# Top-k attention followed by an MLP on one core: all queues in a fixed order, one more step between the stages, half-bank scores, MLP handed out matmul by matmul, centring folded into the first weight

## The chip, the cores and the metric

The kernel runs on one core of a Trainium2 chip. The metric is the device time of one execution in microseconds (us), as the median of several runs. TensorE (PE) does matrix products and transposes, PEld is its weight load, VectorE (DVE), ScalarE (ACT) and GpSimd (POOL) work element by element, and SyncE (SP) issues the DMAs.

## The reference

Two blocks follow each other, all in float32. B = 8 batches, H = 8 heads, S = 576 rows, D = 64 columns per head; the MLP is 512 wide with 2048 hidden columns.

```python
scores = scale * np.matmul(q, k.transpose(0, 1, 3, 2))
kth = np.partition(scores, -top_k, axis=-1)[..., -top_k:-top_k + 1]   # top_k = 32
scores = np.where(scores >= kth, scores, -1000000000.0)
attn = np.exp(scores - np.max(scores, axis=-1, keepdims=True))
attn = attn / (np.sum(attn, axis=-1, keepdims=True) + 1e-09)
x = heads_side_by_side(np.matmul(attn, v))          # (8, 576, 512)
mu, var = mean(x), mean((x - mu) ** 2)               # over the 512 columns
xn = (x - mu) / np.sqrt(var + 1e-06) * g_ln
out = x + np.maximum(xn @ w_ch1, 0.0) @ w_ch2
```

The two weights arrive as float64, which the chip does not compute with, so the kernel builds float32 values from the two 32-bit halves of each number.

## The kernel before

**Units.** Work comes in jobs (a batch and a pair of heads) and in units. A full unit is 128 query rows of both heads of a job; the fifth unit of a job (`rest`) is the last 64 rows of both heads, stacked in one 128-row tile. There are 32 (batch, head pair) combinations, so 160 units, 128 of them full. Batches 0 and 7 are split in two halves (rows 0 to 255, then the rest), each a job of its own, so there are 40 jobs.

**Stages of a unit.** `scores` multiplies queries and keys into two PSUM tiles of two banks each, and ACT copies each tile in one piece of 576 columns to `sc` (L276). `select` runs on DVE: four rounds of the eight largest values (`max`, L288), with three `match_replace` between them (L293). `mask` on POOL (L303, L306) pushes everything under the 32nd value far down. `weigh` is the exp on ACT (L313) with its row sum in `den`. `turn` transposes the weights on PE (L335, L354, L355, L363) and ACT copies them to `pt`. When a group of two or three units is done, `values` multiplies with v (L379), and `place` transposes the result back (L412) and ACT scales it by 1/`den` into the tile `x` (L414). For the `rest` unit the weights themselves are scaled instead (L329).

**MLP.** When a batch (or half) is complete, `mlp_items` gives a list of closures: `stats`, with mean and variance on DVE, the centred tile `xn` on POOL (L451) and its transpose; then 16 `hidden` items of four matmuls (L468); then per tile four `project` items of four matmuls (L483). `fill` pops them in the main loop, in five places per step, evenly over the steps until the next batch ends. The rest rows of two batches make one block of one tile.

**Weights.** `load_weight` handles 32 pieces of 128 x 512 numbers, two per step in the first 16 steps: five DVE operations (L133 to L143), three POOL operations (L135, L144, L146 or L149), one or two on ACT.

**What sets the order.** In step n of the main loop the code traces `scores` of unit n+1, `select` of unit n, `mask` and `weigh` of unit n-1, and `turn` of unit n-2 (and `values` and `place` if it ends a group). That is only a wish: when the program is closed, the framework's scheduler puts each engine's instructions into an order of its own by priority and its estimates. On the chip each engine then takes its queue in that order. PSUM has eight banks: four in `scps`, one in `tpps` for every transpose, three in `mmps` for the products.

Of the kernel before, what the change touches and what calls it, by code (L numbers as in the profile page):

```python
# [15 lines left out]
TOP_K = 32  # L16
# [4 lines left out]
J = 4  # L21
# [7 lines left out]
def kernel(  # L29
# [25 lines left out]

    nc = tc.nc
# [10 lines left out]

    def pool(name, bufs, **kw):
        return ctx.enter_context(tc.tile_pool(name=name, bufs=bufs, **kw))

    GQ = 2 * P + R

    consts = pool("consts", 1)
    ldpool = pool("ld", 2)
    rawpool = pool("raw", 1)
# [10 lines left out]
    xpool = pool("x", 9)  # L86
    rpool = pool("r", 2)
    rowpool = pool("row", 2)
# [3 lines left out]
    tpps = pool("tpps", 1, space=PSUM)  # L92
    mmps = pool("mmps", 3, space=PSUM)

    def const(shape, name):
        return consts.tile(shape, FP32, tag=name, name=name)

# [8 lines left out]
    def load_weight(i):  # L106

        if i < NF:
            c, n0 = i % NC, (i // NC) * DM
            src = w_ch1[c * P : (c + 1) * P, 2 * n0 : 2 * (n0 + DM)]
            dst = w1[:, c, n0 : n0 + DM]
        else:
            f = i - NF
            src = w_ch2[f * P : (f + 1) * P, :]  # L120
            dst = w2[:, f, :]
        raw = rawpool.tile([P, DM, 2], U32, tag="raw", name="raw")
        nc.sync.dma_start(raw[:].rearrange("p n w -> p (n w)"), src)
        lo, hi = raw[:, :, 0], raw[:, :, 1]

        def tmp(name):
            return hpool.tile([P, DM], U32, tag="h", name=name)

        size, sign, power = tmp("size"), tmp("sign"), tmp("power")
        low = hpool.tile([P, DM], FP32, tag="h", name="low")  # L130
        size_f = size[:].bitcast(FP32)
        nc.scalar.mul(low[:], lo, 2.0**-52)
        nc.vector.tensor_scalar(size[:], hi, 0x7FFFFFFF, None, ALU.bitwise_and)  # L133
        nc.vector.tensor_scalar(sign[:], hi, 0x80000000, None, ALU.bitwise_and)
        nc.gpsimd.tensor_scalar(size_f, size_f, HIGH_MAX, HIGH_MIN, ALU.min, ALU.max)  # L135
        nc.vector.tensor_scalar(
            size[:], size[:], 0x38000000, 3, ALU.bitwise_xor, ALU.logical_shift_left
        )
        nc.vector.scalar_tensor_tensor(
            out=size[:], in0=size[:], scalar=0x7FFFFFFF, in1=sign[:],  # L140
            op0=ALU.bitwise_and, op1=ALU.bitwise_or,
        )
        nc.vector.tensor_scalar(power[:], size[:], 0xFF800000, None, ALU.bitwise_and)  # L143
        nc.gpsimd.tensor_tensor(low[:], low[:], power[:].bitcast(FP32), ALU.mult)  # L144
        if i < NF:
            nc.gpsimd.tensor_tensor(low[:], size_f, low[:], ALU.add)  # L146
            nc.scalar.mul(dst, low[:], gcol[:, c : c + 1])
        else:
            nc.gpsimd.tensor_tensor(dst, size_f, low[:], ALU.add)  # L149

    def load_gain():
        grow = const([NC, P], "grow")
        nc.sync.dma_start(grow[:], g_ln.rearrange("(c p) -> c p", p=P))
        ps = tpps.tile([P, 512], FP32, tag="tp", name="gps")
        nc.tensor.transpose(ps[:, 0:NC], grow[:], ident[0:NC, 0:NC])
        nc.vector.tensor_copy(gcol[:], ps[:, 0:NC])

# [3 lines left out]
    slots = [0]  # L161
# [19 lines left out]
    def load(job):  # L181
        b, hp = job.b, job.hp
        ins = {}
        for name, src in (("k", k), ("q", q)):
# [7 lines left out]
            ins[name] = t  # L192
        vb = vpool.tile([P, 2 * J + 1, D], FP32, tag="v", name="vb")
        for hh in range(2):
            rows = v[b, 2 * hp + hh]
# [5 lines left out]
        ins["v"] = vb  # L201
        return ins

    def transpose_heads(ins):
        got = {}
        for name in "kq":
            dst = kqpool.tile([P, S], FP32, tag=name + "T", name=name + "T")
            ps = tpps.tile([P, 512], FP32, tag="tp", name="kqps")
            for c in range(J):
                nc.tensor.transpose(  # L210
                    ps[:, c * P : (c + 1) * P],
                    ins[name][:, c].rearrange("p h d -> p (h d)"),
                    ident[:],
                )
            if name == "k":
                nc.scalar.copy(dst[0:D, 0:JP], ps[0:D, :])
                nc.scalar.copy(dst[D:P, R:S], ps[D:P, :])
            else:
                nc.scalar.copy(dst[:, 0:JP], ps[:])
            got[name] = dst  # L220
            fill()
        ps = tpps.tile([P, 512], FP32, tag="tp", name="kqps")
        for i, name in enumerate("kq"):
            nc.tensor.transpose(
                ps[:, i * R : (i + 1) * R],
                ins[name][0:R, J].rearrange("p h d -> p (h d)"),
                ident[0:R, 0:R],
            )
        nc.scalar.copy(got["k"][0:D, JP:S], ps[0:D, 0:R])
        nc.scalar.copy(got["k"][D:P, 0:R], ps[D:P, 0:R])  # L230
        nc.scalar.copy(got["q"][:, JP:S], ps[:, R : 2 * R])
        return got["k"], got["q"], ins["v"]
# [3 lines left out]
    class Unit:  # L236
        def __init__(self, job, group, qt):
            self.job, self.group, self.qt = job, group, qt
            self.rest = qt == J
            self.tiles = [(0, 1)] if self.rest else [(0,), (1,)]  # L240

# [7 lines left out]
    def scores(u):  # L249
        kT, qT, _ = u.job.heads  # L250
        q0 = u.qt * P
        ql = R if u.rest else P
        pss = [
            scps.tile([P, 2, 512], FP32, tag="scps", name="scps") for _ in u.tiles
        ]
        half = S // 2
        for s in range(2):
            for ps, hs in zip(pss, u.tiles):
                for i, hh in enumerate(hs):
                    r = slice(hh * D, (hh + 1) * D)  # L260
                    pieces = [(0, s * half, half)]
                    if u.rest and hh == 1:
                        pieces = [(0, R + s * half, half - s * R)]
                        if s:
                            pieces += [(half - R, 0, R)]
                    for o, k0, width in pieces:
                        nc.tensor.matmul(  # L267
                            ps[i * R : i * R + ql, s, o : o + width],
                            qT[r, q0 : q0 + ql],
                            kT[r, k0 : k0 + width],  # L270
                            start=True,
                            stop=True,
                        )
        u.sc = scpool.tile([P, 2, S], FP32, tag="sc", name="sc")
        for t, ps in enumerate(pss):
            nc.scalar.copy(  # L276
                u.sc[:, t].rearrange("p (s n) -> p s n", s=2), ps[:, :, 0:half]
            )

    def select(u):  # L280
        nt = len(u.tiles)
        cur = [u.sc[:, t] for t in range(nt)]
        tops, wk = [], {}
        for i in range(TOP_K // 8):
            m = small.tile([P, 2, 8], FP32, tag=f"m{i}", name=f"m{i}")
            tops.append(m)
            for t in range(nt):
# [344 lines left out]
```

## Time and profile before

| what | value |
|---|---|
| median of 3 runs | 2457.5 us (2456.24 to 2458.34) |
| profiled execution | 2458.13 us |
| its span, first to last instruction | 2456.4 us |
| mean granted TensorE clock | 0.879 of 2.4 GHz |
| busy PE / PEld / DVE | 1926.1 / 1012.0 / 1531.4 us |
| busy ACT / POOL | 986.5 / 1284.8 us |

The profile comes from one execution. A busy PE is not PE at its peak: matmuls are pipelined, a record lasts longer than the distance to the next one, and the clock varies. So what a piece of PE work costs is read as the distance between starts in a stretch where PE never waits. Every float32 product shows as two records, every transpose as one.

### The profile page before, as it was taken

The page shows a single profiled execution, that of the slowest core. Times are in us where ns is not written, and L with a number is a line of the kernel's source. Part 1 is how long each engine was busy: PE and PEld are TensorE (multiplying, and loading weights), DVE is VectorE, ACT ScalarE, POOL GpSimd, SP SyncE. Part 2 cuts the span into 40 slices and gives each one's busy share as a digit, 9 for nine tenths or more (in the row PEclk, how much of TensorE's full clock was granted, in tenths as well). Part 3 has the DMA queues.
Part 4 walks back from the last instruction along what each step waited for, and adds up shares of the span by engine and source line. Part 5 has one row for each costly group of instructions (what it writes and reads, how often), then busy time and mean ns, then how long its engine had stood idle before and what let it go on. Part 6 is the DMA issues. An engine that isn't in the chain of part 4 may idle for free. (4 is left out here: it accounts for less than half of the span.)

```text
span 2456.4 us, 23307 instructions
## 1 busy us (share of the span) xinstructions
PE 1926.1 (78%) x7601; PEld 1012.0 (41%) x7601; DVE 1531.4 (62%) x3191; ACT 986.5 (40%) x2330; POOL 1284.8 (52%) x1021
## 2 busy tenths in 40 slices
PE   4544577888799878787799878878699887987888
PEld 2222343543344534333344543333344453445455
DVE  5777777788556786666465685666655585446600
ACT  3443434554333544433333444433343353335421
POOL 4776765667454665455444565445444563344510
PEclk9655887898799989899899898989799898998889
DMA  4222210101000000000000000000000010010000
GB/s 106 79 66 66 75 29 23 25 15 28 10 5 28 20 19 15 15 23 15 14 11 23 24 19 10 15 19 23 9 15 19 23 25 19 19 33 19 1 9 13
DMA packets 125185, 63.13 MB, mean 26 GB/s; under 512 B 106116, under 2 KB 116360, under 8 KB 125064
## 3 DMA queue, kind: packets, MB, share of 16 engines
q1 hardware_dynamic: 125064, 61.64, 9.4%
q8 instruction: 61, 1.00, 0.2%
q14 instruction: 60, 0.49, 0.1%
HBM read 52.17 MB, written 9.44 MB: 25 GB/s over the span
## 5 line engine op out<-in xcount | busy, mean ns | idle before, releaser
L303 POOL TENSOR_SCALAR e<-sc,m 128x576 f32<-128x576 f32 x288 | 642.6, 2231 | 405.6 <-PE tp L363 283.7
L288 DVE MAX8 m<-wk 128x8 f32<-128x576 f32 x864 | 615.9, 748 | 2.3
L468 PE MATMUL hps<-xT,w 128*128 128x512 f32 (+2 forms) x1792 | 598.1, 477 | 9.4 <-ACT h L476 6.2
L288 DVE MAX8 m<-sc 128x8 f32<-128x576 f32 x288 | 207.7, 746 | 590.5 <-ACT sc L276 590.4
L483 PE MATMUL ops<-w,h 128*128 128x512 f32 x1152 | 565.7, 626 | 1.4 <-ACT o L492 1.4
L313 ACT ACTIVATE e<-e,bias 128x576 f32<-128x576 f32 x288 | 223.2, 775 | 719.5 <-POOL e L306 719.3
L293 DVE MATCH_REPLACE8 wk<-m,wk 128x576 f32<-128x576 f32 x576 | 424.1, 743 | 0.0
L306 POOL TENSOR_TENSOR e<-e,sc 128x576 f32<-128x576 f32 x288 | 402.4, 1407 | 16.1
L468 PEld LDWEIGHTS hps<-xT,w 128*128 128x128 f32 x1792 | 316.5, 209 | 181.4 <-issue 154.9
L267 PE MATMUL scps<-kT,qT 64*128 64x288 f32 (+3 forms) x1344 | 292.0, 468 | 44.7 <-ACT sc L276 40.1
L335 PE MATMUL tp<-ident,e 128*128 128x128 f32 x1152 | 203.6, 304 | 157.0 <-ACT pt L346 80.2
L483 PEld LDWEIGHTS ops<-w,h 128*128 128x128 f32 x1152 | 214.6, 202 | 202.9 <-issue 200.0
L335 PEld LDWEIGHTS tp<-ident,e 128*128 128x128 f32 x1152 | 140.8, 153 | 294.2 <-ACT pt L346 136.9
L300 POOL TENSOR_SCALAR bias<-m 128x2 f32<-128x2 f32 (+1 forms) x160 | 41.3, 258 | 371.4 <-DVE m L288 365.7
L379 PE MATMUL av<-pt,vb 128*64 128x256 f32 (+3 forms) x1280 | 211.1, 454 | 8.0 <-ACT pt L357 5.3
L267 PEld LDWEIGHTS scps<-kT,qT 64*128 64x128 f32 (+1 forms) x1344 | 149.9, 192 | 159.5 <-issue 60.9
L293 DVE MATCH_REPLACE8 wk<-m,sc 128x576 f32<-128x576 f32 x288 | 212.3, 742 | 0.0
L346 ACT COPY pt<-tp 128x512 f32<-128x512 f32 x256 | 150.5, 588 | 113.8 <-PE tp L335 112.8
L276 ACT COPY sc<-scps 128x576 f32<-128x576 f32 x288 | 172.3, 639 | 56.2 <-PE scps L267 55.1
L476 ACT ACTIVATE h<-hps 128x512 f32<-128x512 f32 (+2 forms) x224 | 97.7, 443 | 142.9 <-PE hps L468 142.0
L379 PEld LDWEIGHTS av<-pt,vb 128*64 128x64 f32 (+1 forms) x1280 | 91.3, 148 | 124.4 <-issue 78.0
L493 POOL TENSOR_TENSOR o<-o,x 128x512 f32<-128x512 f32 x32 | 40.6, 1269 | 151.8 <-ACT o L492 151.2
(74 smaller groups left out, 1150.9 us busy)
## 6 DMA issues: line engine op xcount, KB each, us to landing
raw<-in_moe_w_ch_dram SPq DMA_DIRECT2D x32, 512.0 KB, 3.9
kin<-in_k_dram SPq DMA_DIRECT2D x80, 128.0 KB, 2.6
qin<-in_q_dram SPq DMA_DIRECT2D x80, 128.0 KB, 2.6
vb<-in_v_dram SPq DMA_DIRECT2D x80, 128.0 KB, 2.2
out_dram<-o SPq DMA_DIRECT2D x32, 256.0 KB, 2.2
kin<-in_k_dram SPq DMA_DIRECT2D x80, 16.0 KB, 2.3
qin<-in_q_dram SPq DMA_DIRECT2D x80, 16.0 KB, 2.3
vb<-in_v_dram SPq DMA_DIRECT2D x80, 16.0 KB, 2.1
```

The source lines that it names most:

```text
L267: nc.tensor.matmul(ps[i * R : i * R + ql, s, o : o + width], qT[r, q0 : q0 + ql], kT[r, k0 : k0 + width], start=True, stop=True,)
L276: nc.scalar.copy(u.sc[:, t].rearrange("p (s n) -> p s n", s=2), ps[:, :, 0:half])
L288: nc.vector.max(m[:, t, :], cur[t])
L293: nc.vector.match_replace(wk[t][:], m[:, t, :], cur[t], LOWEST)
L303: nc.gpsimd.tensor_scalar(u.e[:, t], u.sc[:, t], u.thr[:, t, 7:8], MASKED, ALU.is_lt, ALU.mult)
L306: nc.gpsimd.tensor_tensor(u.e[:, t], u.e[:, t], u.sc[:, t], ALU.add)
L313: nc.scalar.activation(u.e[:, t], u.e[:, t], AF.Exp, bias=u.bias[:, t : t + 1], scale=scale, accum_out=g.den[:, u.col : u.col + 1],)
L335: nc.tensor.transpose(ps[:, c * P : (c + 1) * P], u.e[:, t, k0 : k0 + P], ident[:])
L346: nc.scalar.copy(g.pt[:, t * J : (t + 1) * J, q0 : q0 + P], ps[:].rearrange("p (c n) -> p c n", n=P),)
L379: nc.tensor.matmul(av[h * D : (h + 1) * D, 0 : g.nq], vb[rows, blk, :], g.pt[rows, blk, 0 : g.nq], start=(c == 0), stop=(c == J),)
L468: nc.tensor.matmul(ps[:, 0 : n * P], w1[:, c, f * P : (f + 1) * P], xT[0][:, c, 0 : n * P], start=(c == 0), stop=(c == NC - 1),)
L483: nc.tensor.matmul(out_ps[i][:], hT[f][:, i * P : (i + 1) * P], w2[:, f, :], start=(f == 0), stop=(f == NF - 1),)
```

## The change

Line numbers of the changed kernel are used where its instructions are named.

**Order.** `tc.manual_schedule()` makes the order in which the code is traced the order of every queue. The main loop is written out accordingly. In step n: `weigh` and `turn` of unit n-2, `scores` of n+1 in two halves, `select` of n in four rounds, `mask` of n-1 in two parts, `values` and `place` of a group that ended with n-3, and up to eight places (eleven where heads are transposed) for MLP work. So `weigh` comes one step later than before, and `values` too.

**Scores.** A PSUM tile is now one bank with 288 columns; each half of a unit takes two of them, and ACT copies 288 columns at a time. `scps` has two banks, `tpps` three, `mmps` three.

**MLP.** An item is one matmul instruction with a cost. `give` lays down how much cost each step gets, half of it evenly, half by what PE lacks against DVE in that step. `stats` and the square root are traced outside the list. Centring is gone from the rows: each piece of the first weight becomes g*w minus the column mean of g*w (`mean_of` on PE, `centre` on DVE), and 1/std is applied to the output (`nc.scalar.mul(o, ps, rstd)`). The remaining POOL operation on a tile is the final add. Rest rows of four batches make one block of two tiles.

**Rest rows.** Their weights are no longer scaled before the transpose; the row sums are moved to the right partitions by two small DMAs per unit (`keep_den`) and applied in `place_rest`.

**Weights.** Three DVE operations per piece instead of five, two on ACT, three on POOL; four pieces per step in steps 0 to 2, two in step 3, then one or two.

**Jobs.** Only batch 0 is split, so there are 36 jobs. Batch 7 gives its four tiles and the last two rest tiles together, four steps after its last unit.

```diff
+    ctx.enter_context(tc.manual_schedule())
-    scps = pool("scps", 2, space=PSUM)
-    tpps = pool("tpps", 1, space=PSUM)
+    scps = pool("scps", 2, space=PSUM)
+    tpps = pool("tpps", 3, space=PSUM)
...
+        def split(self):
+            nc.scalar.activation(size_f, self.raw[:, :, 1].bitcast(FP32), AF.Abs)
+            nc.scalar.mul(self.low[:], self.raw[:, :, 0], 2.0**-52)
+            nc.gpsimd.tensor_scalar(size_f, size_f, HIGH_MAX, HIGH_MIN, ALU.min, ALU.max)
+        def bits(self):
...
+        def join(self):
+            nc.gpsimd.tensor_tensor(low[:], low[:], self.power[:].bitcast(FP32), ALU.mult)
+            nc.gpsimd.tensor_tensor(self.dst, self.size[:].bitcast(FP32), low[:], ALU.add)
...
+    def centre(nb):
+        for c in range(NC):
+            w = w1[:, c, nb * DM : (nb + 1) * DM]
+            nc.vector.scalar_tensor_tensor(
+                out=w, in0=w, scalar=gcol[:, c : c + 1], in1=means[nb][:],
+                op0=ALU.mult, op1=ALU.subtract,
+            )
...
     def fill():
-        owed[0] += len(todo) / max(1, slots[0])
-        slots[0] -= 1
-        while todo and owed[0] >= 1.0:
-            owed[0] -= 1.0
-            todo.pop(0)()
+        owed[0] = min(owed[0] + share[0], 6.0)
+        while todo and owed[0] >= todo[0][0] / 2 and (not todo[0][2] or todo[0][2]()):
+            pop()
...
-        if b in (0, B - 1):
+        if b == 0:
...
+        want = {m: max(0.0, kappa * dve_cost(m) - pe_cost(m)) for m in steps}
+        even = need / sum(map(slots, steps))
+        for m in steps:
+            plan[m] = (want[m] * need / total / slots(m) + even) / 2
...
+    for n in range(END):
+        if n in gives:
+            give(n)
+        share[0] = plan.get(n, 0.0)
+        u, nxt, mk, ex = at(n), at(n + 1), at(n - 1), at(n - 2)
+        g = at(n - 3).group if at(n - 3) and at(n - 3).group.last == n - 3 else None
...
+        if ex:
+            weigh(ex, 0)
+        if nxt:
+            scores(nxt, 0)
+        if u:
+            select(u, 0)
+        if mk:
+            mask(mk, 0)
+        piece(0)
+        fill()
+        if g:
+            values(g)
+        if ex and len(ex.tiles) > 1:
+            weigh(ex, 1)
+        fill()
+        if parts:
+            parts[0]()
+        if u:
+            select(u, 1)
+        if mk and len(mk.tiles) > 1:
+            mask(mk, 1)
+        piece(1)
+        fill()
+        if nxt:
+            scores(nxt, 1)
+        fill()
+        if g:
+            place(g)
...
```

**Where rows move.** ACT, one step in the middle of a batch; first before (e is the masked score tile, pt the transposed weights, sc the scores in SBUF, o and x rows of the output and of the MLP's input):

```order
L276 COPY sc<-scps 128x576 x2
L339 COPY pt<-tp 128x8x64
L313 ACTIVATE e,den<-e,bias 128x576 x2
L492 COPY o<-ops 128x512
L357 COPY pt<-tp 64x64 x2
L313 ACTIVATE e,den<-e,bias 128x576 x2
L387 COPY oT<-av 128x320
L414 ACTIVATE x<-xo,den 128x64 x4
```

and ACT in the changed kernel, one whole step in which a group's values are placed:

```order
L404 ACTIVATE e,den<-e,bias 128x576
L367 COPY sc<-scps 128x288 x2
L482 COPY oT<-av 128x320
L404 ACTIVATE e,den<-e,bias 128x576
L431 COPY pt<-tp 128x4x128
L367 COPY sc<-scps 128x288 x2
L486 ACTIVATE x<-xo,den 128x64 x4
L431 COPY pt<-tp 128x4x128
L449 COPY pt<-tp 128x128
```

The exp (L404) now heads each step, belongs to a unit that POOL masked in the step before, and the copies of scores come twice per step.

PE, a step in which values are multiplied (tp is a transpose, ops and hps the two MLP products, av the values, xo the placed rows), before:

```order
L483 MATMUL ops<-w_126,h 128x512 x4
L354 MATMUL tp<-ident,e 64x128
L355 MATMUL tp<-ident,e 128x128
L379 MATMUL av<-pt,vb 64x320 x10
L483 MATMUL ops<-w_126,h 128x512 x4
L412 MATMUL xo<-ident,oT 128x128 x2
L267 MATMUL scps<-kT,qT 128x288
L406 MATMUL xo<-ident,oTr 128x128
L267 MATMUL scps<-kT,qT 128x288 x3
L335 MATMUL tp<-ident,e 128x128 x4
```

and in the changed kernel:

```order
L359 MATMUL scps<-kT,qT 128x288 x2
L589 MATMUL ops<-w_125,h 128x512
L474 MATMUL av<-pt,vb 64x320 x10
L589 MATMUL ops<-w_125,h 128x512
L419 MATMUL tp<-ident,e 128x128 x4
L359 MATMUL scps<-kT,qT 128x288 x2
L589 MATMUL ops<-w_125,h 128x512
L509 MATMUL xo<-ident,oT 128x128 x2
L589 MATMUL ops<-w_125,h 128x512
L419 MATMUL tp<-ident,e 128x128 x4
L589 MATMUL ops<-w_125,h 128x512
L448 MATMUL tp<-ident,e 128x128
```

MLP instructions go out one to three at a time between the attention's pieces, and scores stand at two fixed places of a step.

The end of PE's queue, before, behind the last attention instruction:

```order
L457 MATMUL xps<-ident,xn 128x128 x8
L468 MATMUL hps<-xT,w_125 128x256 x64
L483 MATMUL ops<-w_126,h 128x512 x32
L457 MATMUL xps<-ident,xn 128x128 x4
L468 MATMUL hps<-xT,w_125 128x128 x64
L483 MATMUL ops<-w_126,h 128x512 x16
```

and in the changed kernel:

```order
L559 MATMUL tp<-ident,x 128x128 x16
L572 MATMUL hps<-xT,w_124 128x512 x25
L516 MATMUL xo<-ident,oTr 128x128
L572 MATMUL hps<-xT,w_124 128x512 x39
L589 MATMUL ops<-w_125,h 128x512 x64
L559 MATMUL tp<-ident,r 128x128 x8
L572 MATMUL hps<-xT,w_124 128x256 x64
L589 MATMUL ops<-w_125,h 128x512 x32
```

Six row tiles instead of three stand at the end, behind all attention.

## Rows read from the trace of the kernel before

**Rows 1.** Spans and granted clock of the core (core, span, clock).

```profile
core 0: 2456.4 us, clock 0.879
```

**Rows 2.** Stages, busy us (xinstructions): PE, PEld, DVE, ACT, POOL, PEclk, DMA share, GB/s.

```profile
640.00:900.00 260.00, 227.88 (x962) 117.01 (x960) 165.45 (x347) 113.40 (x275) 140.86 (x110) 0.96 0.08 19
1470.00:1740.00 270.00, 212.80 (x783) 100.09 (x785) 176.33 (x368) 106.21 (x250) 138.18 (x105) 0.89 0.06 15
```

**Rows 3.** Who waited for whom: us in total, times, longest us.

```profile
ACT e L313 <- POOL e L306: 719.3, 243, 8.1
DVE m L288 <- ACT sc L276: 590.4, 79, 28.9
```

**Rows 4.** PE in order of time, 2087 to 2149 us: start, us, engine, line.

```profile
2087.85 2.53 PE L379 MATMUL av<-pt,vb 128*64 128x256 f32 x20
2090.31 3.70 PE L468 MATMUL hps<-xT,w 128*128 128x512 f32 x8
2093.85 0.38 PE L412 MATMUL xo<-ident,oT 128*128 128x128 f32 x2
2094.16 1.24 PE L267 MATMUL scps<-kT,qT 64*128 64x288 f32 x8
2095.33 0.66 PE L335 MATMUL tp<-ident,e 128*128 128x128 f32 x4
2095.82 3.60 PE L468 MATMUL hps<-xT,w 128*128 128x512 f32 x8
...
2116.34 0.70 PE L267 MATMUL scps<-kT,qT 64*128 64x288 f32 x2
2116.97 1.13 PE L468 MATMUL hps<-xT,w 128*128 128x512 f32 x2
```

**Rows 5.** DVE in order of time, first instructions of two units in a row.

```profile
1394.93 1.38 DVE L288 MAX8 m<-sc 128x8 f32<-128x576 f32 x2
...
1404.56 1.40 DVE L288 MAX8 m<-sc 128x8 f32<-128x576 f32 x2
```

**Rows 6.** POOL in order of time, early: one unit's mask and a weight piece.

```profile
27.30 2.26 POOL L303 TENSOR_SCALAR e<-sc,m 128x576 f32<-128x576 f32 x1 [7.51 <-DVE m L288]
29.64 1.40 POOL L306 TENSOR_TENSOR e<-e,sc 128x576 f32<-128x576 f32 x1
31.13 0.61 POOL L135 TENSOR_SCALAR size<-size 128x512 f32<-128x512 f32 x1
...
36.17 1.40 POOL L144 TENSOR_TENSOR low<-low,power 128x512 f32<-128x512 f32 x1
37.64 1.27 POOL L146 TENSOR_TENSOR low<-size,low 128x512 f32<-128x512 f32 x1
39.00 0.61 POOL L135 TENSOR_SCALAR size<-size 128x512 f32<-128x512 f32 x1
```

**Rows 7.** DVE in order of time, its first select: start, us, engine, line.

```profile
17.93 1.53 DVE L288 MAX8 m<-sc 128x8 f32<-128x576 f32 x2 [7.43 <-ACT sc L276]
```

**Rows 8.** Weight operations on DVE: xcount, duration ns min/median/max, first and last start us.

```profile
L136 DVE TENSOR_SCALAR size<-size x32: 400/426/1481, 31.8 to 320.7; 128x512 uint32<-128x512 uint32 x32
...
L139 DVE SCALAR_TENSOR_TENSOR size<-size,sign x32: 666/674/682, 32.8 to 322.9; 128x512 uint32<-128x512 uint32 x32
```

**Rows 9.** The chain that ended last, its end: start, us, what.

```profile
2352.15 3.04 PE av L379 x20
...
2363.80 29.78 PE hps L468 x128
2393.58 27.48 PE ops L483 x64
...
2421.79 1.26 POOL o L493
```

**Rows 10.** ACT's copies out of PSUM, by form: busy us, mean ns, idle before.

```profile
L276 ACT COPY sc<-scps 128x576 f32<-128x576 f32 x288 | 172.3, 639 | 56.2 <-PE scps L267 55.1
L387 ACT COPY oT<-av 128x256 f32<-128x256 f32 x32 | 11.5, 360 | 28.1 <-PE av L379 28.1
```

More of the change, by code (lines that the diff above doesn't have):

```diff
@@ L151, in load_gain @@
+    ready = [False] * (2 * NF)
+    centred = [False] * (DFF // DM)
+    pieces = [Piece(i) for i in range(2 * NF)]
+    gmat = [None]
+    means = {}
     def load_gain():
@@ L247, in __init__, with scores @@
             self.pt = self.den = None
-    def scores(u):
-        kT, qT, _ = u.job.heads
+    def scores(u, s):
+        kT, qT = u.job.T["k"], u.job.T["q"]
         q0 = u.qt * P
         ql = R if u.rest else P
[L253 to L274, printed above, removed]
-        for t, ps in enumerate(pss):
-            nc.scalar.copy(
-                u.sc[:, t].rearrange("p (s n) -> p s n", s=2), ps[:, :, 0:half]
-            )
@@ L297, in mask @@
[L297 to L306 removed]
+        if u.sc is None:
+            u.sc = scpool.tile([P, 2, S], FP32, tag="sc", name="sc")
@@ L308, in weigh, with mask @@
+    def mask(u, t):
+        if t == 0:
+            nt = len(u.tiles)
+            u.bias = small.tile([P, 2], FP32, tag="bias", name="bias")
+            nc.gpsimd.tensor_scalar_mul(u.bias[:, 0:nt], u.top[:, 0:nt, 0], -scale)
+            u.e = epool.tile([P, 2, S], FP32, tag="e", name="e")
+        nc.gpsimd.tensor_scalar(
+            u.e[:, t], u.sc[:, t], u.thr[:, t, 7:8], MASKED, ALU.is_lt, ALU.mult
+        )
+        nc.gpsimd.tensor_tensor(u.e[:, t], u.e[:, t], u.sc[:, t], ALU.add)
     def weigh(u, t):
@@ new lines, in slots, with turns_at, at, pe_cost @@
+    def slots(n):
+        return 8 + (3 if turns_at(n) else 0)
+    def turns_at(n):
+        u = at(n)
+        return u and n == max(u.job.last - 1, u.job.first) and u.job is not jobs[-1]
+    DVE_UNIT, DVE_REST = 9.65, 5.7
+    def at(i):
+        return units[i] if 0 <= i < N else None
+    def pe_cost(n):
+        c = 0.0
+        if at(n + 1):
+            c += 1.25
+        if at(n - 2):
+            c += 1.0 if at(n - 2).rest else 1.65
+        u = at(n - 3)
+        if u and u.group.last == n - 3:
+            c += 3.0
+        if turns_at(n):
+            c += 1.6
+        return c
@@ new lines, in dve_cost, with give @@
+    def dve_cost(n):
+        u = at(n)
+        return 5.0 if u is None else DVE_REST if u.rest else DVE_UNIT
+    plan = {}
+    def give(n):
+        while todo:
+            pop()
+        owed[0] = 0.0
+        for blk in gives[n]:
+            todo.extend(blk.items())
+        after = [m for m in gives if m > n]
+        steps = range(n, min(after) if after else END)
+        need = sum(t[0] for t in todo)
+        kappa = (need + sum(map(pe_cost, steps))) / sum(map(dve_cost, steps))
+        want = {m: max(0.0, kappa * dve_cost(m) - pe_cost(m)) for m in steps}
+        even = need / sum(map(slots, steps))
+        total = sum(want.values())
+        for m in steps:
+            plan[m] = (want[m] * need / total / slots(m) + even) / 2
```

632 lines of the change are left out of this document (371 added, 261 removed).

## The prediction

> **What bounds the kernel now.** I began with the clock and span: 0.879 of full speed over the whole run [rows 1], a first sign that PE is not kept busy. Next the busy times by stage. In a middle batch PE is busy 212.8 of 270 us, DVE 176.3 of 270, POOL less; a batch earlier 227.9 and 165.5 of 260 [rows 2]. No engine is full for a whole stage. The waits say why: DVE sat 590.4 us until ACT had copied scores, up to 28.9 us at a time, and ACT's exp waited 719.3 us for POOL's mask [rows 3]. So the kernel is bound by queues that stop for each other: MLP matmuls go out in bursts while DVE has no scores, then DVE works while PE runs out.
>
> What would bound it if nobody waited comes from a stretch in which PE never pauses, at clock 1.00, taken by distances between starts [rows 4]. Eight records of 512 columns take 3.54 us, 0.43 each once the hand-over is taken off, as the last 64 of the run also do (27.48 / 64) [rows 9]. A unit's scores take 2095.33 - 2094.16 = 1.17 us, four transposes 0.49, two placed rows 0.31, a group's values 2.46 at 256 columns [rows 4] and 3.04 at 320 [rows 9].
>
> A job then costs PE: scores 5 x 1.17 = 5.9; `turn` four units of nine transposes (1.10 each) and one of six (0.73), 5.1; values 2.46 + 3.04 = 5.5; placing 0.7; the ten head transposes 1.2. That is 18.4, and a batch of four jobs 73. Four row tiles of MLP are 128 + 128 records x 0.43 and 16 transposes, 112. A batch is **185 us of PE**. For DVE, a full unit takes 1404.56 - 1394.93 = 9.63 us [rows 5], a rest unit half, 4.8; a batch 16 x 9.63 + 4 x 4.8 = 173, with statistics and reciprocals about **178 us of DVE**. Middle batches take 260 to 270 now [rows 2]. The gap of some 80 us per batch is what the change can reach.
>
> **The change part by part.** I follow the order of stages; a step is one turn of the main loop.
>
> *Weights and start, steps 0 to 15.* DVE's first select started at 17.93 us [rows 7]; now one piece of weight operations (two of 0.43 us and one of 0.67, 1.5 [rows 8]) stands before it, so 19.4. POOL paces these steps. A masked tile costs 31.13 - 27.30 = 3.8 us, a full unit with its bias 8.0; a piece 0.7 + 1.47 + 1.36 = 3.5 [rows 6]. Step 0 (four pieces, no mask) takes 14.2; steps 1 and 2 take 8.0 + 14.2 = 22.2 each; step 3 takes 15.0; steps 4 to 15 hold 18 pieces and twelve masks, two of them of rest units, 152. That ends at 244. Steps 16 to 22 hold five full and two rest units on DVE, 58, so step 23 begins at **about 301**. The saved DVE operations (two of five per piece) are hidden behind POOL; the added ones, four centring operations per quarter of the first weight, 0.67 us each by the same row, fit in too (9.63 + 4 x 1.5 + 2.7 = 18 against 22). If that cover fails, DVE is late next. One row speaks against me: a weight operation on DVE that normally takes 426 ns once took 1481 [rows 8], and such operations now meet a busy POOL more often. The Trainium skill ("SBUF — State Buffer", Who interferes with whom) has such DVE operations and POOL share a port which one holds for a whole instruction while the other waits. By that rule at its worst, every one of them at 1.48 us, steps 0 to 15 would be DVE's and end some 35 us later; no run here shows how often it will happen.
>
> *Batches.* The MLP of one batch is spread over the 20 steps of the next, starting four steps after its last unit. Steps 23 to 42 carry only the second half of batch 0 (58 us of MLP, 131 us of PE in all), so DVE sets them: 178. Steps 43 to 82 are two batches of PE, 2 x 185 = 370. Steps 83 to 102 also carry the first two rest tiles: hidden at 256 columns 29.78, two projected tiles 27.48 [rows 9], eight transposes 1, so 58 more: 243. Steps 103 to 142 are 370. In steps 143 to 162 the last 17 units end, 0.87 x 73 of attention and 112 of MLP: 175. Sum so far: 301 + 178 + 370 + 243 + 370 + 175 = 1637.
>
> *Tail.* Behind all attention stand four tiles and two rest tiles, 112 + 58 = 170 us, where before three tiles stood there (29.78 + 27.48 for two [rows 9], and one more). With ACT's copy, POOL's add at 1.26 [rows 9] and the store, 175. This is the one place where the change costs: some 84 us more of PE alone at the end (three tiles at 28), though the work is the same and only lies elsewhere. Ideal sum: **1812 us**.
>
> *What hides and what is added on the busy engines.* Dropping POOL's centring, the scaling of rest weights and the fifth weight operations costs or gains nothing after step 15, since PE sets the time; they loosen POOL and ACT. Copying scores in halves: 576 columns took 639 ns, 256 took 360 [rows 10], so 288 take about 390, two halves 780, on ACT 0.14 x 288 = 41 us more over the run, beside PE. Half-bank scores on PE: eight records in 1.17 us now go in two goes of four; two records alone took 0.63 [rows 4], which is the only row near a short go. Two goes cost between 1.17 (they overlap as now) and four such pairs, 2.5; between these I take 1.26, two goes at 0.63, since a go has two heads that overlap as the eight did, and keep +1.3 per unit (150 us over the 115 units where PE sets the time) for the high end. The two small DMAs per rest unit have a whole step before their use. On SP they stand behind an exp and ahead of the next loads, which are issued a job early, so a wait of a few us there meets no one.
>
> *Waits that are left.* In the written-out order an exp is a step behind its mask, so POOL's 8.0 us and DVE's 9.6 overlap with slack of 1.6 per step, and a score half stands some 4 to 5 us of PE work ahead of its reader. With rest steps shorter on DVE (4.8) than on POOL (8.0) the slack swings by 3 us within a job. I charge 0.2 us per step for hand-overs and 0.1 for the halves on the 120 steps where PE sets the time: 36. And PE's clock: stages with PE at 80 to 88% busy ran at 0.89 to 0.96 [rows 2]; a denser queue should be at or near the upper value, I take 0.95 on the 1158 us of steps 43 to 162: + 61. Sum 1812 + 36 + 61 = 1909 as a span; the profiled execution was 1.7 us longer than its span and 0.6 above the median, so **1910 us**.
>
> **The rivals.**
>
> *The clock stays where it is.* Every step still has a dozen hand-overs between PE and ACT. If PE keeps pausing for fractions of a microsecond and the clock stays at the 0.88 of [rows 1], the 1158 us become 1316: 1812 + 158 + 36 + 2 = **2008**. For it: the stage at 0.89 had PE 79% busy [rows 2], which is not idle. Against it: the stretch of [rows 4] ran at 1.00 with the same mixture of short and long matmuls. The Trainium skill ("TensorE: Matmul & The Clock Gate", A second HAM failure mode) describes this case, small idles between groups that make the clock swing; the trace agrees in so far as stages with gaps show 0.89.
>
> *Half of the waiting survives.* PE idled 530 of 2456 us; if half of that share stays on the 1158 us (125) with the clock at 0.88: 1812 + 36 + 158 + 125 = **2131**. For it: the plan of MLP per step uses fixed costs, and no queue can swap. Against it: the rows that wait most now [rows 3] are waits within one step, and those are the ones that the extra step removes.
>
> *Slower than before: ACT's queue is held at its head.* The exp is the first of ACT's step, and everything PE waits for (score banks, transposed weights) lies behind it. Today the exp waits 719.3 / 243 = 3.0 us for POOL each time [rows 3]. If POOL's mask is late by that much at the exp in spite of the step in between, both exps of a step (2 x 3.0) stop ACT, then PE, then DVE's scores: 6 us x 143 steps = 858, **2768**. The break-even is (2458 - 1910) / 160 = 3.4 us per step. It needs POOL to fall behind by a full step; at 8.0 us of POOL against 9.6 of DVE it should catch up, so I give it little.
>
> *Better than the sum of stages.* If hand-overs hide in PE's queue and the clock is at 1.0, the ideal 1812 is left, or less where MLP starts earlier than I think.
>
> **How the numbers follow.** Forecast, stages near PE's sum with clock between 0.93 and 0.97: 0.63. Clock stays: 0.20. Half the waiting: 0.07. Held queue, slower: 0.04. Better: 0.06. The range goes from the ideal sum to the third case, 1812 to 2130, which leaves out the slow case and the outer parts of the second and fourth, and takes in the high end for the halves (1910 + 150 = 2060). 0.2% is about 5 us, what a measurement of this kernel can tell from no change; only a mixture of the third rival and the held queue comes near 2457, so faster 0.95, same 0.01, slower 0.04.
>
> **What would show it.** In the changed profile: step 23 near 300 us; DVE waiting for score copies under 100 us in total against 590; the exp's wait for POOL nearly gone; a middle batch in 190 to 200 us with PE's records dense and the clock over 0.93; a tail of 175 us with PE alone. The forecast is wrong if a middle batch takes over 210 us; then it matters whether PE was waiting (hand-overs), slow (clock), or DVE had no scores. It is wrong in its first part if step 23 starts after 330.

## The result, and the profile after

The changed kernel took **1931.99 us** (median of 4 runs, 1929.94 to 1932.22) against 2457.92 for the one before in the same session: a ratio of 0.7859, 95% interval 0.7845 to 0.7873. Forecast were 1910, between 1812 and 2130. The direction and the size held. Three terms of the sum did not: one was too dear by 61 us, two too cheap by 39 and 37, so that the sum came as close as it did was partly luck.

Span and granted clock of the changed kernel, against 2456.4 us and 0.879 in [rows 1]:

```profile
core 0: 1927.8 us, clock 0.959
```

Its stages by windows cut at starts of steps (busy us and, in brackets, instructions of PE, PEld, DVE, ACT, POOL; then PE clock, DMA share, GB/s), to be read against [rows 2]:

```profile
21.00:280.00 259.00, 153.02 (x637) 87.55 (x635) 255.95 (x427) 124.59 (x313) 223.67 (x175) 0.76 0.30 85
280.00:337.80 57.80, 55.17 (x239) 25.93 (x238) 57.48 (x120) 32.12 (x89) 46.53 (x38) 1.00 0.09 24
337.80:518.10 180.30, 158.07 (x765) 87.84 (x766) 179.51 (x381) 107.02 (x301) 141.61 (x111) 0.91 0.10 24
518.10:910.40 392.30, 388.39 (x1630) 179.23 (x1631) 360.38 (x762) 223.97 (x588) 282.57 (x219) 1.00 0.09 24
910.40:1162.40 252.00, 249.04 (x1013) 125.23 (x1012) 182.12 (x383) 121.81 (x315) 144.77 (x110) 1.00 0.08 21
1162.40:1562.20 399.80, 395.19 (x1668) 183.22 (x1667) 360.28 (x761) 230.20 (x602) 285.94 (x221) 1.00 0.09 24
1562.20:1751.20 189.00, 186.19 (x771) 86.21 (x769) 150.89 (x320) 104.14 (x271) 128.32 (x102) 1.00 0.05 14
1751.20:1927.80 176.60, 168.57 (x474) 87.61 (x472) 1.93 (x7) 25.67 (x50) 8.84 (x7) 0.99 0.03 11
```

Each stage now has one full engine. In the first and third lines it is DVE (255.95 of 259.00 us, 179.51 of 180.30), from step 43 on PE (388.39 of 392.30) at clock 1.00. Before, a middle batch had PE busy for 213 of 270 us and DVE for 176 [rows 2].

The waits that answer to [rows 3] (us in total, times, longest):

```profile
DVE m L377 <- ACT sc L367: 90.8, 24, 10.4
...
ACT e L404 <- POOL e L397: 5.9, 5, 3.3
```

DVE's wait for score copies fell from 590.4 to 90.8 us, the exp's wait for the mask from 719.3 to 5.9. PE in the middle of a PE-bound stage, in order of time (start, us), read like [rows 4] by distances between starts:

```profile
600.31 1.88 PE L572 MATMUL hps<-xT,w 128*128 128x512 f32 x4
602.12 0.76 PE L359 MATMUL scps<-kT,qT 64*128 64x288 f32 x4
602.80 3.06 PE L474 MATMUL av<-pt,vb 128*64 128x320 f32 x20
605.79 1.13 PE L572 MATMUL hps<-xT,w 128*128 128x512 f32 x2
606.76 0.60 PE L419 MATMUL tp<-ident,e 128*128 128x128 f32 x4
607.19 1.02 PE L572 MATMUL hps<-xT,w 128*128 128x512 f32 x2
608.15 0.76 PE L359 MATMUL scps<-kT,qT 64*128 64x288 f32 x4
```

No row has idle time before it. Two MLP records here take 0.96 us until the next start (606.76 - 605.79 and 608.15 - 607.19), where 0.43 per record [rows 9] makes 0.86 for two; four scores, half a unit, take 0.68 (602.80 - 602.12).

The start is where the sum was furthest off. Durations of the weight operations on DVE (xcount, ns min/median/max, first and last start):

```profile
L160 DVE TENSOR_SCALAR size<-size x32: 407/456/1497, 19.1 to 266.0; 128x512 uint32<-128x512 uint32 x32
L163 DVE SCALAR_TENSOR_TENSOR size<-raw,size x32: 693/1635/1777, 19.6 to 266.9; 128x512 uint32<-128x512 uint32 x32
L167 DVE TENSOR_SCALAR power<-size x32: 426/1110/1389, 20.3 to 268.6; 128x512 uint32<-128x512 uint32 x32
```

The operation with two inputs took 666 to 682 ns before [rows 8], and now 1635 at the median. The means of the three, from the costliest groups (busy us, mean ns, idle before), of the changed kernel and then of two counterparts before:

```profile
L163 DVE SCALAR_TENSOR_TENSOR size<-raw,size 128x512 uint32<-128x512 uint32 x32 | 46.8, 1464 | 1.1
...
L167 DVE TENSOR_SCALAR power<-size 128x512 uint32<-128x512 uint32 x32 | 32.0, 1001 | 1.1
...
L160 DVE TENSOR_SCALAR size<-size 128x512 uint32<-128x512 uint32 x32 | 20.0, 626 | 8.4 <-POOL size L155 8.2
```

```profile
L136 DVE TENSOR_SCALAR size<-size 128x512 uint32<-128x512 uint32 x32 | 14.6, 456 | 74.8 <-POOL size L135 74.8
...
L143 DVE TENSOR_SCALAR power<-size 128x512 uint32<-128x512 uint32 x32 | 13.8, 430 | 0.0
```

One such operation on DVE, and what POOL did meanwhile (start, us):

```profile
36.47 1.63 DVE L163 SCALAR_TENSOR_TENSOR size<-raw,size 128x512 uint32<-128x512 uint32 x1
```

```profile
34.86 1.27 POOL L173 TENSOR_TENSOR low<-low,power 128x512 f32<-128x512 f32 x1 [1.09 <-DVE power L167]
36.21 1.34 POOL L174 TENSOR_TENSOR w<-size,low 128x512 f32<-128x512 f32 x1
37.52 1.05 POOL L155 TENSOR_SCALAR size<-size 128x512 f32<-128x512 f32 x1
```

POOL's sum had begun at 36.21 and ended at 37.55; DVE's operation began in its middle and ended at 38.10, 0.55 us after it, a little less than the operation's own time.

The whole trace repeats this. In 29 of the 32 cases L163 began while one of POOL's tensor_tensor operations or its L155 was running, and each time it ended 0.54 to 0.55 us after that operation: 0.98 us long behind L155, 1.63 to 1.65 behind L173 or L174, 1.77 to 1.78 behind the second mask operation (L397). One that began early in the first mask operation (L394) took 1.11. Two began with none under way, or in the last 0.06 us of one, and took 0.69, among them the first, which was ahead of POOL by 0.01 us; there POOL's operation took 1.15 us, where the one before it had taken 0.61:

```profile
19.58 0.69 DVE L163 SCALAR_TENSOR_TENSOR size<-raw,size 128x512 uint32<-128x512 uint32 x1
```

```profile
18.47 0.61 POOL L155 TENSOR_SCALAR size<-size 128x512 f32<-128x512 f32 x1 [5.64 <-ACT size L153]
19.59 1.15 POOL L155 TENSOR_SCALAR size<-size 128x512 f32<-128x512 f32 x1 [0.51 <-ACT size L153]
```

Before, the counterpart L139 never met such an operation. It began with POOL at rest in 20 cases, and in the other 12 while the first mask operation (L303) had already been running for 0.8 us or more, which did not lengthen it:

```profile
32.79 0.67 DVE L139 SCALAR_TENSOR_TENSOR size<-size,sign 128x512 uint32<-128x512 uint32 x1
```

```profile
31.84 2.44 POOL L303 TENSOR_SCALAR e<-sc,m 128x576 f32<-128x576 f32 x1
```

So "POOL is busy" is not enough. What counts here is which POOL operation is under way when DVE's begins. The trace of before shows this too, in an operation with one input that [rows 8] leaves out, one of the two that the change saves: 10 of its 32 cases took 1.48 to 1.62 us, each of them behind a POOL tensor_tensor.

```profile
L134 DVE TENSOR_SCALAR sign<-raw x32: 410/418/1619, 28.6 to 318.5; 128x512 uint32<-128x512 uint32 x32
```

### The profile page after: what moved, and what is told of

It reads as the page before. It is cut to its first block, busy times and chain, and to the rows that moved or that the text cites. A ratio compares the mean times of both kernels' runs of the same rounds, so it can differ in the third digit from the quotient of the medians.

```text
span 1927.8 us, 22931 instructions
## 1 busy us (share of the span) xinstructions
PE 1761.7 (91%) x7209; PEld 867.9 (45%) x7209; DVE 1550.5 (80%) x3156; ACT 977.3 (51%) x2541; POOL 1266.3 (66%) x992
## 4 chain that ended last, share of the span: by engine, by line
PE 61%; DVE 22%; issue 11%; ACT 3%; POOL 3%; DMA 1%; SPq 1%; POOLq 0%; ACTq 0%
PE ops L589 19%; PE hps L572 19%; DVE m L377 9%; PE scps L359 8%; DVE wk L382 7%; PE av L474 7%; PE tp L419 5%; DVE size L163 2%; DVE power L167 1%; PE tp L301 1%; POOL e L394 1%; DVE size L160 1%; POOL e L397 1%; PE xo L509 1%; DVE w L212 1%
## 5 line engine op out<-in xcount | busy, mean ns | idle before, releaser
L394 POOL TENSOR_SCALAR e<-sc,m 128x576 f32<-128x576 f32 x288 | 639.0, 2219 | 330.5 <-PE tp L448 100.1
L572 PE MATMUL hps<-xT,w 128*128 128x512 f32 (+1 forms) x1408 | 580.5, 533 | 30.7 <-ACT xT L564 18.0
L397 POOL TENSOR_TENSOR e<-e,sc 128x576 f32<-128x576 f32 x288 | 406.1, 1410 | 24.1
L572 PEld LDWEIGHTS hps<-xT,w 128*128 128x128 f32 x1408 | 240.5, 193 | 189.3 <-issue 138.4
L367 ACT COPY sc<-scps 128x288 f32<-128x288 f32 x576 | 204.9, 403 | 204.9 <-PE scps L359 114.6
L359 PE MATMUL scps<-kT,qT 64*128 64x288 f32 (+3 forms) x1344 | 258.7, 456 | 28.9 <-ACT sc L367 19.5
L377 DVE MAX8 m<-sc 128x8 f32<-128x576 f32 x288 | 203.5, 743 | 91.0 <-ACT sc L367 90.8
L589 PEld LDWEIGHTS ops<-w,h 128*128 128x128 f32 x1152 | 192.2, 191 | 169.5 <-issue 167.0
L404 ACT ACTIVATE e<-e,bias 128x576 f32<-128x576 f32 x288 | 224.8, 780 | 6.4 <-POOL e L397 5.9
L359 PEld LDWEIGHTS scps<-kT,qT 64*128 64x128 f32 (+1 forms) x1344 | 109.5, 180 | 231.0 <-issue 55.1
L419 PE MATMUL tp<-ident,e 128*128 128x128 f32 x1152 | 182.7, 283 | 25.8 <-ACT e L404 25.4
L474 PE MATMUL av<-pt,vb 128*64 128x320 f32 (+3 forms) x1280 | 182.6, 422 | 0.0
L584 ACT ACTIVATE h<-hps 128x512 f32<-128x512 f32 (+1 forms) x176 | 92.3, 524 | 120.4 <-PE hps L572 120.0
L474 PEld LDWEIGHTS av<-pt,vb 128*64 128x64 f32 (+1 forms) x1280 | 81.9, 138 | 107.4 <-issue 54.6
L482 ACT COPY oT<-av 128x256 f32<-128x256 f32 (+1 forms) x64 | 25.6, 400 | 149.2 <-PE av L474 148.9
```

Of the source, the lines that this page charges most:

```text
L359: nc.tensor.matmul(ps[i * R : i * R + ql, o : o + width], qT[r, q0 : q0 + ql], kT[r, k0 : k0 + width], start=True, stop=True,)
L367: nc.scalar.copy(u.sc[:, t, s * HALF : (s + 1) * HALF], ps[:, 0:HALF])
L377: nc.vector.max(m[:, t, :], u.cur[t])
L394: nc.gpsimd.tensor_scalar(u.e[:, t], u.sc[:, t], u.thr[:, t, 7:8], MASKED, ALU.is_lt, ALU.mult)
L397: nc.gpsimd.tensor_tensor(u.e[:, t], u.e[:, t], u.sc[:, t], ALU.add)
L404: nc.scalar.activation(u.e[:, t], u.e[:, t], AF.Exp, bias=u.bias[:, t : t + 1], scale=scale, accum_out=g.den[:, col : col + 1],)
```

## Experiments

Theory: the fixed order and the step between mask and exp remove the waits; what is left is PE's own work, dearer than counted because it changes often between MLP and attention; the late start comes from DVE and POOL meeting in the weight operations. The rivals stand with each run. What the folded centring, the lighter rest rows and the fewer jobs bring by themselves was not run. "Steps 43 to 82" means the distance between the first selects of units 43 and 83: 392.2 us in the changed kernel.

**The order left to the scheduler.**

```diff
-    ctx.enter_context(tc.manual_schedule())
```

> The changed kernel without the fixed order: the framework's scheduler orders each queue, all else as changed. Theory, the fixed order is what keeps PE filled: 2100 us or more, PE idle over 250 us against 166, DVE waiting over 300 us for score copies against 91. Rival, the extra step between stages, the banks and the lighter POOL carry the gain whatever the order: under 2000 us.

Measured: 2216.42 us, ratio 0.9033 (0.8999 to 0.9068). Clock and waits:

```profile
core 0: 2216.7 us, clock 0.917
```

```profile
ACT e L402 <- POOL e L395: 624.2, 184, 12.1
DVE m L375 <- ACT sc L365: 263.9, 92, 8.9
```

With the same source but a free order the exp waits for the mask nearly as long as before [rows 3]. PE is idle for 323 us (2216.7 less 1893.3 busy), over the 250 foretold; DVE's wait is smaller than the 300 us foretold. Taken in this order, all other parts of the change together bring 240 us and the fixed order on top of them another 284, more than half.

**The exp back in the step of its mask**, in the fixed order: `weigh` stands behind each `mask`, as before the change.

```diff
-        if ex:
-            weigh(ex, 0)
...
             mask(mk, 0)
+            weigh(mk, 0)
...
-            weigh(ex, 1)
...
             mask(mk, 1)
+            weigh(mk, 1)
```

> The exp goes back into the step of its mask, right behind it in the trace order, as before the change; all else as changed. Theory, the step between mask and exp keeps the head of ACT's queue free: ACT's exp waits for POOL 300 to 900 us in total against 6, PE and DVE wait behind it, 2100 to 2700 us. Rival, the fixed order and three transpose banks suffice, since PE has MLP work in its queue: 1915 to 1960 us.

Measured: 2067.03 us, ratio 0.8424 (0.8395 to 0.8454), under the range given. Waits, and steps 43 to 82 by window:

```profile
ACT e L404 <- POOL e L397: 495.7, 199, 11.1
...
DVE m L377 <- ACT sc L367: 160.3, 56, 8.5
```

```profile
560.10:993.20 433.10, 406.19 (x1654) 188.74 (x1654) 361.62 (x762) 225.45 (x600) 285.61 (x220) 0.96 0.09 22
```

This is the rival of the held queue, made on purpose. The exp waits 2.5 us each time, 199 times, and yet it costs 135 us, not hundreds: in the window PE is not busy for 27 of 433 us (4 of 392 in the changed kernel), and its clock falls from 1.00 to 0.96, some 17 us more. The rest of ACT's waiting does not reach PE. That MLP work already in PE's queue covers it fits this, but no run takes that work away.

**MLP four matmuls at a time**: each item of `hidden` and `project` issues four instructions.

```diff
-                    lambda f=f, c=c: hidden(f, c),
+                    lambda f=f, c=c: [hidden(f, c + i) for i in range(4)],
...
-                for c in range(NC)
+                for c in range(0, NC, 4)
```

> MLP handed out four matmuls at a time with four times the cost per item. Theory, PE is full in the middle and pays about 0.1 us each time it changes between MLP and attention: half as many changes save about 5 us per batch, 1890 to 1915 us. Rival, bursts of 3.4 us hold up scores and transposes: DVE's wait for score copies rises well over 91 us and the time is 1940 us or more.

Measured: 1961.12 us, ratio 0.7993 (0.7968 to 0.8018). Distances between starts over steps 43 to 82: MLP records 226.1 us against 238.9, as foretold; but score halves 0.79 us each against 0.68 (62.0 against 53.5 us in all), four transposes 0.51 against 0.47, and PE idle 11.1 us against 3.7. The rival was right on the total: what the longer bursts save is lost on what waits behind them. Its sign, DVE waiting well over 91 us, came only weakly (109.9).

**Scores in one go**, with four banks for scores, one left for transposes, three for products.

```diff
-        pss = [scps.tile([P, 512], FP32, tag="scps", name="scps") for _ in u.tiles]
+        pss = [scps.tile([P, 2, 512], FP32, tag="scps", name="scps") for _ in u.tiles]
...
-    tpps = pool("tpps", 3, space=PSUM)
+    tpps = pool("tpps", 1, space=PSUM)
```

> A unit's scores in one go into tiles of two banks (four banks in all), one transpose bank instead of three; all else as changed. Theory, half-bank scores cost PE 1.34 us per unit against 1.17 and the third transpose bank is worth little: 3 us per batch less, 1905 to 1925 us. Rival, what the half banks buy is the transpose banks: with one, PE waits for ACT's copy at each of three transposes per unit, 0.5 us or more each, 1990 us or more.

Measured: 1999.72 us, ratio 0.815 (0.8123 to 0.8177). The new wait:

```profile
PEld tp L452 <- ACT pt L435: 144.4, 125, 10.2
```

A unit's scores fell to 1.19 us, but four transposes rose from 0.47 to 0.66: with a single bank they wait for ACT's copy out of it. The rival was right.

**Scores in one go with two banks for transposes and two for products** (the edit is against the run before).

```diff
-    tpps = pool("tpps", 1, space=PSUM)
-    mmps = pool("mmps", 3, space=PSUM)
+    tpps = pool("tpps", 2, space=PSUM)
+    mmps = pool("mmps", 2, space=PSUM)
```

> Scores in one go in four banks, two transpose banks and two product banks. Theory, the loss of whole scores came from the single transpose bank: with two, PE's waits for ACT's copies go, scores cost 1.19 us per unit instead of 1.34, 1910 to 1930 us. Rival, scores as late or as long as this, or too few product banks, hold up DVE or PE: 1950 us or more.

Measured: 1933.21 us, ratio 0.7868 (0.7852 to 0.7884), the changed kernel's time. Over steps 43 to 82 scores take 1.16 us per unit against 1.35, some 8 us less over 40 units, transposes 0.45 for four, and MLP records 231.0 us against 238.9; but the two placed rows of a group (`xo`) rose from 0.24 to 1.19 us, 15 us in all, behind ACT's reading of a product bank:

```profile
PE xo L513 <- ACT x L490: 61.6, 53, 9.0
```

So the halves cost PE about 0.2 us per unit, and the bank that pays for undoing them takes it back.

**Batch 7 split in halves**, as before the change.

```diff
-        if b == 0:
+        if b in (0, B - 1):
...
-            if b % 4 == 3:
+            if b % 4 == 3 and j.groups[-1].qts[-1] == J:
```

> Batch 7 is split into two halves of jobs as before the change, so that half of its MLP is done before the end and four row tiles are left for the tail instead of six. Theory, PE is full from step 43 on, so the work only moves: four more head transposes and 175 us of tail become about 120, the steps before grow by as much, 1925 to 1945 us. Rival, the tail is extra time in which DVE is idle, and 55 us less of it come off: 1875 to 1900 us.

Measured: 1941.52 us, ratio 0.7902 (0.7886 to 0.7918), about 10 us over the changed kernel. Unit 159 starts at 1792.6 instead of 1720.6: the work at the end only moves ahead of the last unit.

**The shifted word in PSUM.** L163's second input (and the output of the operation ahead of it) goes to a PSUM bank; the arithmetic is the same.

```diff
+            ps = product("bits")[:].bitcast(U32)
             nc.vector.tensor_scalar(
-                size[:], size[:], 0x38000000, 3, ...
+                ps, size[:], 0x38000000, 3, ...
             )
             nc.vector.scalar_tensor_tensor(
-                out=size[:], in0=self.raw[:, :, 1], scalar=0x80000000, in1=size[:],
+                out=size[:], in0=self.raw[:, :, 1], scalar=0x80000000, in1=ps,
```

> The shifted word of each weight piece goes into a PSUM bank and is read from there, so the joining operation on DVE (L163) has one SBUF input instead of two; the same operations on the same data otherwise. Theory, that operation waits for POOL because both read SBUF over something shared: its mean falls from 1464 to about 700 ns, the shift loses its own waits too, 32 x 0.8 = 25 us less on DVE, step 23 at 310 to 325 instead of 338, 1905 to 1920 us. Rival, the long durations come from something else (the uint32 type, the interleaved input), so it stays at 1.4 us and 1932.

Measured: **1901.57 us** (1900.05 to 1904.54), ratio 0.7743 (0.7730 to 0.7756), 30 us under the changed kernel, a little under the range given, and the fastest of the runs that compute the whole result. The operation's durations, in the same view as above, and the window that answers to the first one of the changed kernel:

```profile
L164 DVE SCALAR_TENSOR_TENSOR size<-raw,bits x32: 686/687/702, 19.2 to 239.0; 128x512 uint32<-128x512 uint32 x32
```

```profile
21.00:250.00 229.00, 145.63 (x612) 86.55 (x612) 220.63 (x425) 123.11 (x303) 209.13 (x174) 0.76 0.34 94
488.50:880.80 392.30, 388.37 (x1630) 179.19 (x1630) 360.35 (x762) 224.22 (x588) 282.53 (x219) 1.00 0.09 24
```

The operation has its old time again, in all 32 cases, while POOL does the same work. The gain on DVE is more than this operation's 25 us (46.8 to 22.0): the next one, with a single input in SBUF, falls from 32.0 to 20.6 as well.

```profile
L168 DVE TENSOR_SCALAR power<-size 128x512 uint32<-128x512 uint32 x32 | 20.6, 643 | 1.1
```

The one ahead of it, now writing to PSUM, loses its long cases as foretold but takes 668 to 696 ns in all 32, so it gains nothing at the mean (681 against 626). Step 23 starts at 308.2 instead of 337.8, and steps 43 to 82 are unchanged: all of the gain is at the start.

**POOL's join left out.** The two POOL operations that add the low half to each weight are left out of the computation; ACT copies the high half.

```diff
-            nc.gpsimd.tensor_tensor(low[:], low[:], self.power[:].bitcast(FP32), ALU.mult)
-            nc.gpsimd.tensor_tensor(self.dst, self.size[:].bitcast(FP32), low[:], ALU.add)
+            nc.scalar.copy(self.dst, self.size[:].bitcast(FP32))
```

> POOL's two tensor_tensor per weight piece are left out and ACT copies the high half into place instead: the low half of each weight is left out of the computation. Theory, DVE is slowed by a busy POOL in steps 0 to 22: POOL has 64 x 1.4 us less to do, the joining operation on DVE falls under 1000 ns though its operands are the same, step 23 starts at 300 to 315, 1895 to 1910 us. Rival, DVE is full there by its own work: its operations stay as long, step 23 stays near 338.

Measured: 1899.23 us, ratio 0.7730 (0.7714 to 0.7745); step 23 at 307.6. Here it is POOL that changes and DVE that speeds up:

```profile
L163 DVE SCALAR_TENSOR_TENSOR size<-raw,size x32: 691/836/1768, 19.0 to 236.1; 128x512 uint32<-128x512 uint32 x32
```

The same instruction, both inputs in SBUF, falls from a median of 1635 to 836 ns. Those that still meet a POOL operation keep the old pattern: 13 behind L155 take 0.98 us, the two behind the second mask operation 1.76 to 1.77. From both sides, the excess of this operation needs both of its inputs in SBUF and certain POOL operations under way.

**Two further tries with the shifted word in PSUM** (POOL's join back in place): MLP two matmuls at a time, and the MLP laid evenly over the steps.

```diff
-                    lambda f=f, c=c: hidden(f, c),
+                    lambda f=f, c=c: [hidden(f, c + i) for i in range(2)],
```

> The shifted word goes through a PSUM bank as in the run before, and the MLP is given out two matmuls at a time. Theory (every change between MLP records and attention work costs PE about 0.1 us): about 95 of the 190 changes per two batches go, some 9 us per two batches, 20 to 28 us over steps 43 to 162, so 1875 to 1885 us. Rival (longer bursts delay the score halves and turn the gain into waits, as with four at a time): 1897 to 1930 us, DVE waiting over 100 us for score copies.

```diff
-            plan[m] = (want[m] * need / total / slots(m) + even) / 2
+            plan[m] = even
```

> The shifted word goes through a PSUM bank, and the MLP is laid evenly over the steps instead of half by what PE lacks against DVE. Theory (PE is the bound and the queues follow their order with slack): the plan shifts work by a few us between neighbouring steps, no item is gained or lost, 1897 to 1912 us. Rival (the share by need is what keeps DVE fed in rest and transposing steps): DVE waits over 150 us for score copies and the time is over 1925 us.

Measured: 1903.51 us, ratio 0.7763 (0.7751 to 0.7774), and 1906.46, ratio 0.7774 (0.7761 to 0.7787). In the first, MLP records took 235.4 us over steps 43 to 82 against 238.9, less than foretold, and score halves (57.3 against 53.5) and transposes (36.2 against 33.0) ate more than that. By the distances, a burst of two records takes 0.94 us at the mean in the changed kernel, `ops` bursts of four here 1.81, bursts of eight with four at a time 3.53 to 3.55: with 0.43 per record, about 0.09 per burst at the mean, whatever its length. But it is not one price. Of 188 bursts in steps 43 to 82 of the changed kernel 40 cost nothing beyond 0.43 per record, all of them ahead of transposes; 130 cost about 0.10; 18 cost about 0.20, among them all ten ahead of values. With whole scores and two transpose banks 78 of 167 cost nothing, nearly all of those ahead of placed rows among them. So what comes next matters, and the layout of the banks or of the scores; which of these, and why the other records pay for what longer bursts save, is open. The first is no faster than the version it starts from. Its time lies in the rival's range, but not for the rival's reason: DVE waited 81.9 us for scores, less than 90.8. In the second, steps 43 to 82 took 396.5 us instead of 392.3 and DVE waited 96.5 us for scores against 90.8: the share by need is worth some 5 us.

## Why the prediction was right or wrong

In stages, forecast and measured:

| stage | forecast, ideal | measured | difference |
|---|---|---|---|
| start to step 23 | 301 | 337.8 | +37 |
| steps 23 to 42 | 178 | 180.3 | +2 |
| steps 43 to 82 | 370 | 392.2 | +22 |
| steps 83 to 102 | 243 | 252.0 | +9 |
| steps 103 to 142 | 370 | 399.9 | +30 |
| steps 143 to 162 | 175 | 189.0 | +14 |
| tail | 175 | 176.6 | +2 |
| hand-overs, halves, clock | 97 | in the rows above | -97 |

- **The waits were read right.** DVE's wait for scores was foretold under 100 us (90.8) and the exp's nearly gone (5.9). That the extra step does this, and not the order alone, the run with the exp moved back shows (496 us again, 135 us slower); that the order is needed as well, the run with a free order.
- **The step that failed: "the saved DVE operations are hidden behind POOL" and "POOL paces these steps".** DVE was full there (256 of 259 us), POOL was not, and step 23 came at 338, past the 330 that the prediction had named as its own refutation. By means the 32 operations of L163 rose by 32 x (1464 - 674 ns [rows 8]) = 25 us, those of L167 by 32 x (1001 - 430) = 18, those of L160 by 32 x (626 - 456) = 5: 48 us more of DVE, against 37 by which the start was late. The one row that the prediction held against its sum [rows 8] was the sign, and L134 in the trace of before, shown above, was a stronger one. With the word in PSUM the start was 308, close to 301, but even then DVE was the fuller engine (220.6 of 229 us, POOL 209.1): the number for the start without that contention was near, its owner was not POOL. The Trainium skill ("SBUF — State Buffer", Who interferes with whom) says that a DVE instruction with two SBUF inputs contends with a POOL instruction that reads SBUF, and one with at most one SBUF input outside the two-port modes does not; both runs agree, 687 ns with one input in PSUM, 1635 with two in SBUF, but the 12 cases of L139 during the mask operation L303, which reads SBUF, took 0.67 us and do not. The estimate worked out beside that rule, 35 us later, was the better number (step 16 began at 276.7, 33 us after the 244 of the sum), but not by its own split. It comes out at 35 if the two one-input operations of a piece take 1.48 us and the two-input one stays at 0.67; they added 23 us, and the two-input one 25.
- **The clock term, 61 us, was not there.** Steps 43 to 162 ran at 1.00, not 0.95. The rival "the clock stays" (2008) falls with it. The Trainium skill's case of small idles between groups ("TensorE: Matmul & The Clock Gate", A second HAM failure mode) did not come up where PE was full, but with the exp moved back, PE idle 6% of the time, the clock was 0.96.
- **The term for hand-overs and halves, 36, was too small**: PE's stages exceed their ideal by 22 + 9 + 30 + 14 = 75 us with hardly a pause (4 of 392). In steps 43 to 82 the 512 MLP records took some 19 us more than the 0.43 each that [rows 4] and [rows 9] gave, in 190 bursts. The prediction had taken the hand-over off the 3.54 us of eight records and then charged 0.2 us per step for it; nearly five bursts per step at 0.09 make over 0.4, because the change cuts the bursts of eight into twos and fours. Scores took 1.35 per unit where 1.26 was taken: about 4 us more over 40 units. Transposes gave some back (0.47 against 0.49). So these two errors, -61 and +39, leave -22, and the start's +37 with +2 each for the DVE stage and the tail makes +19 in the span; the rest of the miss of 22 us is that the median lies 4.2 us over the profiled span, where 1.1 had been counted (1.7 less 0.6). That -61 and +76 nearly cancel is luck.
- **The work at the end** was costed right (176.6 against 175), and splitting batch 7 again moved it without gain.
- **The held queue** was priced at its whole wait. Made on purpose it cost about 135 us for 496 us of waiting, so the price of 858 us took every wait on ACT for one on PE; even with this held queue the kernel was 16% faster than before, not slower.
- **Half the waiting surviving** (2131) did not come: PE pauses for 1% of the middle stages. **Better than the sum of stages** did not come either.

## What to carry to other kernels

Where a kernel is bound by queues that stop for each other, sum each engine's own work per stage at the distances seen in a stretch without pauses: the largest sum is what to measure a new order against, and here the span came within 7% of it. Read those distances from bursts as short as the new order will issue, since here a burst cost 0.09 us at the mean, however short. And before taking an operation on DVE at its old price, look which POOL operations will now run beside it: a few outliers in the row of durations can be the normal case of the changed kernel.

## What the runs showed of the hardware

- A 128x512 DVE operation with two SBUF inputs took 674 ns before, 1635 at the median in the changed kernel, 836 with two of POOL's operations per piece gone, and 687 with one input in PSUM. In 29 of 32 cases it began behind a running POOL operation and ended 0.54 to 0.55 us after it; 12 cases before, begun well into POOL's L303, were not lengthened.
- Operations with a single SBUF input stretch too: L167 took 1001 ns at the mean, its counterpart before 430; L134 before took 418 at the median and 1619 at most.
- A burst of 512-column float32 records cost about 0.09 us at the mean beyond 0.43 per record, whether it held two, four or eight: 0, 0.10 or 0.20, in part by what came next.
- TensorE's granted clock was 1.00 of 2.4 GHz in every window from step 43 to the tail (0.99 there), with a new kind of matmul every two or four records and PE busy for 99% of steps 43 to 82.
